# Attention followed by a token and channel mixer on one core: seven block products for the third batch pair's first channel product, thirteen tile pairs, and a new instruction order

## The chip, the cores and the metric

One core of one Trainium2 chip runs the whole program. The time is device microseconds (us) of one execution. The kernel before takes 354.57 us, the median of three runs (353.96 to 354.92). The trace that is read below is one further, profiled execution.

## What is computed

There are 8 batches, 12 heads, 448 rows of the sequence and 64 columns a head. The attention has no softmax: the scores are clipped at zero, squared and multiplied with V. Its output is the input of a mixer: a token product over the sequence with a clip and a second token product, added to the input, then a channel product from 768 to 1536 columns, a clip, and a channel product back to 768, added to its input.

```python
scores = scale * np.matmul(q, k.transpose(0, 1, 3, 2))
attn = np.maximum(scores, 0.0) ** 2 / S
x = attn @ v                                  # heads side by side: (8, 448, 768)
h = np.maximum(x.transpose(0, 2, 1) @ w_tok1, 0.0) @ w_tok2
u = x + h.transpose(0, 2, 1)
out = u + np.maximum(u @ w_ch1, 0.0) @ w_ch2
```

## The kernel before, in words

**Attention** goes over 24 groups of four heads (three groups a batch). A group's K, Q and V come in by six DMAs on the POOL queue (`ldk`, `ldq`, `ldv`, two halves each, line 289), into one of four buffers. K and Q are turned either on TensorE (`T`, groups 0 to 9, with evictions `cp`) or, from group 10 on, by VectorE copies (`ik`, `iq`) and one crossbar transpose on the SP queue (`x`). A score chunk `S{group}.{0..6}` is four 64x64 matmuls (line 431) into two PSUM banks; two evictions `r` clip it (ScalarE at line 267 or VectorE at line 269); one instruction `q` squares it in SBUF (line 441, always VectorE); a value piece `V` is four matmuls (line 458) that accumulate over the seven chunks. Two evictions `xe` close a group.

**Token mixing** of a group turns its rows (on TensorE, `X`, with evictions `xc`, or from group 5 on by a crossbar transpose `xd`, line 481), multiplies twice (`t1`, line 502; `t2`, line 511), with an eviction `rt` between, and adds the group back in (`u`, VectorE, line 515).

**The first channel product** of a batch is twelve products `C1` of six 448-column matmuls (line 565), each evicted and clipped by `c1e` into `r2`, a ring of ten tiles. Two batches make a pair, seven tiles of 128 rows. For the fourth pair (`WIDE = (3,)`) `channel1_wide` computes it in another way: per pair of 128-column blocks seven products `E` of three matmuls (line 645) take the place of the 24 matmuls of two blocks and two batches. It needs four weight sums `sa` (line 609) and four sums of the input `tb` (line 629), both on VectorE. The weight sums are written over the attention's square buffers, `sq_all`, and so wait until the last value piece has read them; the input sums lie over `kqT_all`. Three of the products are saved (`v`, ScalarE or VectorE) and added later (`v` at line 661, with a clip `z`).

**The second channel product** works on tiles of 128 rows. A single tile, `C2`, takes two times twelve matmuls of 384 columns (line 746) and two evictions `c2e` that also add the residual. Two tiles of a pair in `PAIRS` take seven products `D` of six matmuls (line 802) in place of 48, with four sums `ds` (line 788) and seven evictions `de` (lines 773 and 818). The residual, `u` turned back, comes through crossbar transposes `ub` on the SP queue (line 523), but for the batches in `RESPE`, where three 128-column matmuls for each half tile (line 750) add it on TensorE. Stores `st` leave on the SP queue.

**The order** is written out: the string `ORDER` names every step once, and each engine gets its steps in that sequence. `:A` or `:D` puts an eviction on ScalarE or VectorE, digits after a colon are the PSUM banks, `fill:bank*count` is a run of dummy matmuls, and `:g` on a DMA holds a load back until the last crossbar transpose has landed, or a transpose until the last load has. No cost table or due time stands in the kernel.

Of the kernel before, what the change touches and what calls it, by code (L numbers as in the profile page):

```python
# [12 lines left out]
HOLD = 1  # L13
NSIDE = 2
FUSED = set()
# [56 lines left out]
ldk1.1 ldf.1 ldf.0 ldk0.1:g cast1.1:A ldk0.0:g ldq1.1:g cast0.0:A ldk1.0 cast1.0:D ldv0.0 ldq1.0 ident fill:0*21  # L72
T0.1:0 cast0.1:D fill:1*4 T0.0:1 cp0.1:A cp0.0:D ldv0.1 ldk2.1 fill:2*12 S0.0:23 ldq2.0 ldk2.0:g r0.0.0:A S0.2:45
r0.0.1:D r0.2.1:A wt1.0 ldq2.1:g S0.5:67 S0.6:01 r0.5.0:D S0.4:23 q0.0:D S0.1:56 r0.5.1:A r0.2.0:A T1.0:74 r0.1.1:A
r0.6.1:D q0.2:D r0.1.0:A S0.3:16 cp1.1:D r0.4.1:D ldv1.1:g ldv1.0 ldq3.0:g cp1.0:A S1.2:54 r0.6.0:A S1.0:73 q0.1:D
r0.4.0:A r0.3.1:D ldq3.1:g r1.0.1:D r0.3.0:A ldk3.1 fill:0*3 V0.0:02 wt2 V0.1 r1.2.0:A S1.1:16 r1.0.0:A ldk3.0 S1.3:53
q0.5:D r1.1.0:A q0.3:D fill:7*4 S1.4:71 V0.2 r1.3.1:A ldv2.1:g q0.4:D V0.3 wt1.1:g V0.4 q1.0:D r1.2.1:A ldv3.0 S1.6:34
ldv2.0 r1.4.1:A V0.5 r1.1.1:A r1.3.0:A q0.6:D q1.2:D q1.3:D fill:1*5 V0.6 r1.6.1:A r1.6.0:A q1.1:D ldq4.1 r1.4.0:A
T2.0:16 xe0.0:A S1.5:54 cp2.1:A fill:3*5 V1.0:37 xe0.1:A cp2.0:D ldq4.0 V1.1 r1.5.1:A q1.4:D fill:0*8 S2.2:01 r1.5.0:D
V1.2 ldk4.1 r2.2.0:A S2.1:62 r2.2.1:D q1.5:D r2.1.1:A r2.1.0:A q1.6:D V1.3 S2.0:54 r2.0.0:A V1.4 fill:1*6 V1.5 S2.6:10  # L80
r2.0.1:D X0.1:2 X0.0:6 r2.6.1:A V1.6 r2.6.0:A S2.3:54 xc0.1:D S2.4:02 xc0.0:D xe1.1:A T3.0:16 r2.4.1:A ldk4.0 q2.2:D
r2.4.0:D r2.3.1:A wc1.0 q2.0:D X1.1:7 ldv3.1:g xc1.1:A t1.0.1:2 rt0.1:D t1.0.0:0 t1.1.1:4 t2.0.1:7 xe1.0:A cp3.1:D
rt0.0:A t2.0.0:2 q2.1:D u0.1:D r2.3.0:A S2.5:30 q2.4:D cp3.0:A q2.3:D r2.5.0:A ldk5.1 rt1.1:D ldq5.0:g V2.0:65 ldq5.1
V2.1 S3.0:71 r2.5.1:A V2.2 r3.0.0:A r3.0.1:A q2.5:D X1.0:3 q2.6:D V2.3 ldk5.0:g V2.4 xc1.0:A S3.4:07 ldq6.1:g S3.3:41
u0.0:D V2.5 t1.1.0:3 r3.4.0:A V2.6 ldq7.0:g r3.3.1:D T4.0:02 r3.3.0:A rt1.0:A S3.1:43 xe2.1:D xe2.0:A X2.0:1 cp4.0:D
X2.1:6 cp4.1:A t2.1.1:5 xc2.0:D t2.1.0:0 xc2.1:D r3.1.0:A r3.1.1:A u1.1:D t1.2.0:2 t1.2.1:1 wc1.1 ldv4.1:g r3.4.1:A
q3.3:D S4.1:46 rt2.0:A rt2.1:A u1.0:D r4.1.0:A S4.2:35 q3.4:D S3.2:72 r4.2.1:A t2.2.0:1 ldv4.0 u2.0:D t2.2.1:0
r4.2.0:A C1.0.0a:4 u2.1:D S3.5:53 q3.1:D S3.6:10 r3.2.1:A q3.0:D r3.2.0:A r3.5.0:D C1.0.4:2 r3.5.1:A r3.6.1:A C1.0.0
V3.0:73 r4.1.1:A ldq6.0 c1e0.4:A q3.2:D r3.6.0:A S4.3:05 c1e0.0:D V3.1 S4.5:62 r4.3.1:A V3.2 r4.3.0:A T5.0:14 V3.3
q4.1:D S4.4:50 r4.5.0:A cp5.1:A q4.2:D q3.6:D V3.4 q3.5:D C1.0.5:6 V3.5 r4.5.1:D S4.0:42 V3.6 cp5.0:A r4.4.1:D  # L90
ldk7.0:g C1.0.1a:1 C1.0.2a:0 r4.0.1:D ldk6.1:g c1e0.5:D xe3.0:A r4.0.0:D xe3.1:D C1.0.1 r4.4.0:A S4.6:27 S5.2:65
S5.0:43 r4.6.1:A C1.0.2 ldv5.0 q4.0:D r4.6.0:D q4.6:D X3.0:7 r5.0.1:D C1.0.9:2 c1e0.2:A r5.2.1:A C1.0.7:0 V4.0:53
r5.2.0:A c1e0.1:A q4.5:D S5.3:61 r5.0.0:D c1e0.9:D C1.0.11:4 q5.0:D ldk6.0:g V4.1 c1e0.7:A S5.4:20 xc3.0:D r5.3.1:D
# [118 lines left out]
def kernel(ctx: ExitStack, tc: tile.TileContext, q: bass.AP, k: bass.AP, v: bass.AP, moe_w_tok1: bass.AP, moe_w_tok2: bass.AP, moe_w_ch1: bass.AP, moe_w_ch2: bass.AP, out: bass.AP):  # L212
    nc = tc.nc
# [716 lines left out]
```

## Time and profile before

| what | value |
|---|---|
| three runs, median (lowest to highest) | 354.57 us (353.96 to 354.92) |
| the profiled execution's own time | 353.8 us |
| its span | 352.0 us |
| TensorE clock granted | 1.00 throughout |
| TensorE busy | 343.8 us, 98% of the span |
| VectorE busy | 296.0 us, 84% |
| ScalarE busy | 201.0 us, 57% |
| GpSimd busy (it issues the loads) | 91.4 us, 26% |
| DMA moved | 49.85 MB |

The span runs from the first to the last instruction; 1.8 us of the execution lie around it. The profiled execution is 0.8 us below the median of the three runs. PE stands for TensorE's matmuls, PEld for its weight loads, DVE for VectorE, ACT for ScalarE, POOL for GpSimd and SP for the engine that issues most transposes and the stores. A matmul's duration holds its latency, so that what a matmul costs in a stream is read from the start of one to the start of the next, or from a long run of them.

### The profile page before, as it was taken

How to read it: one execution, taken by the hardware profiler on the slowest of the kernel's cores; microseconds unless marked ns; L12 is line 12 of the kernel's file. 1: busy time of each engine (PE TensorE's matmuls, PEld its weight loads, DVE VectorE, ACT ScalarE, POOL GpSimd, SP SyncE). 2: the span in 40 equal slices, each digit the busy share in tenths (PEclk: the TensorE clock that was granted, in tenths of full speed). 3: DMA queues.
4: the chain of work that ended last, by engine and by line, in shares of the span. 5: the costliest groups of instructions: out<-in, count | busy, mean ns of one | idle time of the engine just before them, and what ended most of it. 6: DMA issues, size and time to landing. Idle time of an engine off the chain costs nothing.

```text
span 352.0 us, 8801 instructions
## 1 busy us (share of the span) xinstructions
PE 343.8 (98%) x3547; PEld 190.9 (54%) x3547; DVE 296.0 (84%) x570; ACT 201.0 (57%) x429; POOL 91.4 (26%) x156
## 2 busy tenths in 40 slices
PE   8899999999999999999999999999999999999995
PEld 7475454455565455554555555555545565555563
DVE  2999999889769899897986888879689998968972
ACT  3999879687763586656345237475757621344200
POOL 8883291166046100910244221231000000000000
PEclk9999999999999999999999999999999999999999
DMA  8999999989999998999889997996784540617336
GB/s 150 168 177 188 198 129 196 189 108 150 149 168 168 239 164 112 123 155 174 146 150 203 138 194 108 170 176 91 123 129 40 149 96 4 114 28 165 74 93 167
DMA packets 95626, 49.85 MB, mean 142 GB/s; under 512 B 69536, under 2 KB 92128, under 8 KB 95584
## 3 DMA queue, kind: packets, MB, share of 16 engines
q0 software_dynamic: 24352, 21.47, 43.4%
q1 hardware_dynamic: 70992, 27.60, 43.2%
q8 instruction: 28, 0.46, 0.5%
q10 hardware_dynamic: 240, 0.20, 0.2%
q14 instruction: 14, 0.11, 0.1%
HBM read 43.38 MB, written 11.01 MB: 155 GB/s over the span
## 4 chain that ended last, share of the span: by engine, by line
PE 93%; DVE 2%; DMA 1%; POOL 1%; issue 1%; ACT 0%; POOLq 0%
PE m_ps L565 24%; PE w_ps L802 22%; PE acc_ps L458 10%; PE sc_ps L431 9%; PE w_ps L645 7%; PE t_ps L502 6%; PE m_ps L746 6%; PE h_ps L511 5%; PE kqT_ps L390 1%; DMA x_sb<-xT 1%; POOL raw_all L289 1%; DVE sq_all L441 1%; PE fill_ps L899 1%; PE x_ps L493 1%; DVE sq_all L269 1%
## 5 line engine op out<-in xcount | busy, mean ns | idle before, releaser
L267 ACT ACTIVATE sq_all<-sc_ps 128x448 bf16<-128x448 f32 x243 | 118.3, 566 | 36.2 <-PE sc_ps L431 29.4
L441 DVE TENSOR_TENSOR sq_all<-sq_all 128x896 bf16<-128x896 bf16 x168 | 98.8, 617 | 5.4 <-ACT sq_all L267 5.0
L565 PE MATMUL m_ps<-uT_sb,wc 128*128 128x448 bf16 x432 | 90.3, 353 | 0.0
L269 DVE TENSOR_SCALAR sq_all<-sc_ps 128x448 bf16<-128x448 f32 x93 | 55.8, 618 | 10.0 <-PE sc_ps L431 9.6
L565 PEld LDWEIGHTS <-wc 128*128 128x128 bf16 x432 | 39.9, 98 | 42.3 <-issue 9.1
L458 PE MATMUL acc_ps<-sq_all,raw_all 64*64 64x448 bf16 x672 | 58.3, 357 | 0.2
L431 PE MATMUL sc_ps<-kqT_all 64*64 64x448 bf16 x672 | 53.0, 353 | 1.3 <-ACT kqT_all L273 0.9
L267 ACT ACTIVATE r_sb<-m_ps 128x448 bf16<-128x448 f32 (+3 forms) x78 | 32.8, 451 | 37.3 <-PE m_ps L565 36.9
L289 POOL DMA_DIRECT2D raw_all<-in_v_dram x48 | 29.2, 614 | 69.7 <-DMA u_sb<-uT_sb 22.2
L289 POOL DMA_DIRECT2D raw_all<-in_k_dram x48 | 29.7, 622 | 48.7 <-DMA x_sb<-xT 16.2
L802 PE MATMUL w_ps<-wd,r2d 128*128 128x384 bf16 x198 | 36.8, 326 | 0.0
L289 POOL DMA_DIRECT2D raw_all<-in_q_dram x46 | 28.5, 636 | 31.0 <-DVE side_all L409 19.4
L802 PEld LDWEIGHTS <-r2d 128*128 128x128 bf16 x264 | 25.2, 98 | 19.1 <-issue 2.1
L515 DVE TENSOR_TENSOR uT_sb<-h_ps,xT 128x448 bf16<-128x448 f32 x48 | 29.3, 619 | 6.9 <-PE h_ps L511 6.4
L458 PEld LDWEIGHTS <-raw_all 64*64 64x64 bf16 x672 | 20.0, 105 | 22.0 <-issue 16.1
L431 PEld LDWEIGHTS <-kqT_all 64*64 64x64 bf16 x672 | 23.2, 105 | 15.7 <-issue 6.7
L773 DVE TENSOR_TENSOR out_sb<-w_ps,u_sb 128x384 f32<-128x384 f32 x44 | 23.9, 552 | 7.5 <-PE w_ps L802 7.3
L802 PEld LDWEIGHTS <-r_sb 128*128 128x128 bf16 x198 | 19.0, 98 | 14.4 <-issue 1.8
L746 PE MATMUL m_ps<-wc,r_sb 128*128 128x384 bf16 (+2 forms) x156 | 26.4, 314 | 0.0
L502 PE MATMUL t_ps<-x_sb,wt 128*128 128x256 bf16 (+1 forms) x216 | 24.7, 261 | 0.7 <-DMA x_sb<-xT 0.7
L511 PE MATMUL h_ps<-wt,r_sb 128*128 128x448 bf16 x96 | 24.8, 354 | 0.0
L802 PE MATMUL w_ps<-wc,r_sb 128*128 128x384 bf16 x132 | 24.6, 326 | 0.0
(71 smaller groups left out, 336.6 us busy)
## 6 DMA issues: line engine op xcount, KB each, us to landing
out_dram<-out_sb SPq DMA_DIRECT2D x54, 192.0 KB, 3.2
raw_all<-in_k_dram POOLq DMA_DIRECT2D x48, 112.0 KB, 4.9
raw_all<-in_v_dram POOLq DMA_DIRECT2D x48, 112.0 KB, 4.8
raw_all<-in_q_dram POOLq DMA_DIRECT2D x46, 112.0 KB, 5.2
wc<-in_moe_w_ch_dram POOLq DMA_DIRECT2D x2, 1152.0 KB, 11.2
wc<-in_moe_w_ch_dram POOLq DMA_DIRECT2D x3, 768.0 KB, 12.5
u_sb<-uT_sb SPq DMA_TRANSPOSE x42, 3.2
side_all<-in_q_dram SPq DMA_DIRECT2D x2, 224.0 KB, 3.9
```

What stands on the lines that cost most here:

```text
L267: nc.scalar.activation(out, ps, AF.Relu)
L269: nc.vector.tensor_scalar(out=out, in0=ps, scalar1=0.0, scalar2=None, op0=ALU.max)
L289: return nc.gpsimd.dma_start(out=raws[t][s % NR][64 * half:64 * (half + 1)], in_=src[b, h0:h0 + 2].rearrange('e (p c) d -> p e (c d)', c=KC))
L431: nc.tensor.matmul(o.ps[e][64 * half:64 * (half + 1), :S], lhsT=lhsT, rhs=rhs, start=True, stop=True, skip_group_check=True)
L441: sq_ops[s, c] = [add(Op(f'q{s}.{c}', 'DVE', lambda o: nc.vector.tensor_tensor(out=buf, in0=buf, in1=buf, op=ALU.mult), ev))]
L458: nc.tensor.matmul(o.ps[half][64 * e:64 * (e + 1), :S], lhsT=r[rows, e, c * D:(c + 1) * D], rhs=sq[rows, e, :], start=c == 0, stop=c == KC ...
L502: nc.tensor.matmul(o.ps[:, j, :], lhsT=wt1[:, c, j * 128:(j + 1) * 128], rhs=x_sb[:, p0:p1, c, :], start=c == 0, stop=c == 3)
L511: nc.tensor.matmul(o.ps[:, :S], lhsT=r1[:, j, a * 128:(a + 1) * 128], rhs=wt2[:, j, :], start=j == 0, stop=j == JC - 1)
L515: nc.vector.tensor_tensor(out=uTs[bb % 2][:, 2 * i + a, off:off + S].rearrange('n (c p) -> n c p', c=KC), in0=t2.ps[:, :S].rearrange('n (p ...
L565: nc.tensor.matmul(ps[:, :S], lhsT=wc1[:, g, e * 128:(e + 1) * 128], rhs=uT[:, g, off:off + S], start=g == 0, stop=g == CC - 1)
L746: nc.tensor.matmul(o.ps[:, :size], lhsT=r2[:, e, r2_tile(n)], rhs=wc2[:, e, cols], start=e == 0, stop=e == EC - 1)
L802: nc.tensor.matmul(o.ps[:, :C2], lhsT=lhs[:, e], rhs=rhs[:, e], start=holder is None and e == 0, stop=e == H2 - 1, skip_group_check=True)
```

## The change

Four settings change, and the whole `ORDER` string is new. `WIDE = (2, 3)` gives the third batch pair (batches 4 and 5) the seven block products too: 24 steps `C1` and 24 steps `c1e` go, 42 steps `E2`, four `tb2` and the evictions that belong to them come. Its seven tiles are ready only after all attention. `PAIRS` goes from 11 pairs to 13; the single tiles left are 0 and 27. `RESPE` is empty, so that batch 0's residual comes by six crossbar transposes in place of 18 matmuls on TensorE. `HOLD` and `FUSED` had no effect in the kernel before. A square `q` can now be put on ScalarE; 68 of the 168 are. The dummy matmuls go from 68 to 56.

```diff
-RESPE = {0}
-PAIRS = ((3, 4), (5, 6), (7, 8), (10, 11), (12, 13), (14, 15), (17, 18), (19, 20), (21, 22), (23, 24), (25, 26))
-WIDE = (3,)
+RESPE = set()
+PAIRS = ((1, 2), (3, 4), (5, 6), (7, 8), (9, 10), (11, 12), (13, 14), (15, 16), (17, 18), (19, 20), (21, 22), (23, 24), (25, 26))
+WIDE = (2, 3)
...
-st16.64 sa0:D st13.64 V22.6 V23.6 D17.2:0 rt21.0:A ds17.2:D t2.20.0:7 xe22.1:A sa1:D t2.21.0:1 st15.0 xe22.0:A
+V23.0:14 r23.5.0:A q23.5:D q23.6:A V23.1 V22.6 V23.2 xe22.1:A xe22.0:A V23.3 tb2.0:D V23.4 V23.5 V23.6 st9.64 sa1:D
...
-        sq_ops[s, c] = [add(Op(f'q{s}.{c}', 'DVE', lambda o: nc.vector.tensor_tensor(out=buf, in0=buf, in1=buf, op=ALU.mult), ev))]
+        def square(o):
+            if o.on == 'ACT':
+                nc.scalar.activation(buf, buf, AF.Square)
+            else:
+                nc.vector.tensor_tensor(out=buf, in0=buf, in1=buf, op=ALU.mult)
+        sq_ops[s, c] = [add(Op(f'q{s}.{c}', 'DVE', square, ev))]
...
-        free = [sc[s, c] for s in range(NS - NQ, NS) for c in range(KC)]
+        free = sums_use or [sc[s, c] for s in range(NS - NQ, NS) for c in range(KC)]
...
-            old = hold.get(e - 4, raw_free)
+            old = saved[turn - 4] if turn >= 4 else raw_free
...
-            hold[e] = [ops_of(v2), ops_of(v5), ops_of(v3)]
+            saved.append([ops_of(v2), ops_of(v5), ops_of(v3)])
+            readers += [p4, p5, p6, p7]
+        sums_use[:] = readers
```

The last three pieces let the fourth pair use the input sums' and the saved products' buffers after the third pair.

The order moves at three places that matter below. The first is ScalarE at the start of the program. The names are those of the tiles: `sq_all<-sc_ps` is a clip `r` out of PSUM, `sq_all<-sq_all` a square, `kqT_all<-kqT_ps` an eviction `cp`, `xT<-acc_ps` an eviction `xe`. Before:

```order
L273 ACT_TABLE_LOAD
L273 ACTIVATE raw_all<-side_all 64x448 x2
L273 ACTIVATE kqT_all<-kqT_ps 128x896
L267 ACTIVATE sq_all<-sc_ps 128x448 x6
L273 ACTIVATE kqT_all<-kqT_ps 128x896
L267 ACTIVATE sq_all<-sc_ps 128x448 x14
L468 ACTIVATE xT_64<-acc_ps 128x448
```

And now (the lines of the changed file stand a few further down):

```order
L278 ACT_TABLE_LOAD
L278 ACTIVATE raw_all<-side_all 64x448
L278 ACTIVATE kqT_all<-kqT_ps 128x896
L272 ACTIVATE sq_all<-sc_ps 128x448 x4
L446 ACTIVATE sq_all<-sq_all 128x896
L272 ACTIVATE sq_all<-sc_ps 128x448 x4
L446 ACTIVATE sq_all<-sq_all 128x896
L272 ACTIVATE sq_all<-sc_ps 128x448 x8
L476 ACTIVATE xT_64<-acc_ps 128x448
```

Squares stand between the clips, and one eviction `cp` and one cast have moved to VectorE. One table load stands at the head of either list and there is none further down.

The second place is VectorE around the end of attention, where the weight sums are made (`side_all<-wc` and `sq_all<-wc`, `sa`). `r2d` is the sum buffer of a tile pair, `uT_sb<-h_ps,xT` a step `u`. Before:

```order
L441 TENSOR_TENSOR sq_all<-sq_all 128x896
L609 TENSOR_TENSOR side_all<-wc_69 128x2304
L788 TENSOR_TENSOR r2d_1_92<-r2d_0_91,r_sb 128x768
L609 TENSOR_TENSOR sq_all<-wc_69 128x2304
L788 TENSOR_TENSOR r2d_3_94<-r_sb,r2d_1_92 128x768
L515 TENSOR_TENSOR uT_sb_80<-h_ps,xT_66 128x448
```

And now, with `kqT_all<-uT_sb` the input sums `tb2` and `r_sb<-w_ps,raw_all` the additions to saved products:

```order
L448 TENSOR_TENSOR sq_all<-sq_all 128x896 x6
L637 TENSOR_TENSOR kqT_all<-uT_sb_79 128x1344
L617 TENSOR_TENSOR sq_all<-wc_69 128x2304
L637 TENSOR_TENSOR kqT_all<-uT_sb_79,kqT_all 128x1344
L617 TENSOR_TENSOR sq_all<-sq_all,wc_69 128x2304
L617 TENSOR_TENSOR side_all<-wc_69 128x2304
L670 TENSOR_TENSOR r_sb<-w_ps,raw_all 128x448 x2
```

Before, tile pairs' sums lie between the weight sums, and 60 matmuls of the tile pairs 17 and 19, with the last token products, stand on TensorE between the last value piece and the first `E`. Now the weight sums follow the last squares at once, and TensorE has five products `E` and one `t1` between the last value piece and the first product that needs two weight sums.

The third place is the SP queue at the start. `u_sb<-uT_sb` is a residual transpose `ub`, `x_sb<-xT` a step `xd`, `kqT_all<-side_all` a step `x`. Before:

```order
L343 DMA side_all<-in_q_dram 64x2x448 x2
L481 DMA_TRANSPOSE x_sb_76<-xT_66 128x8x128
L523 DMA_TRANSPOSE u_sb<-uT_sb_79 128x4x128
L481 DMA_TRANSPOSE x_sb_75<-xT_64 128x8x128
L481 DMA_TRANSPOSE x_sb_76<-xT_65 128x8x128
L523 DMA_TRANSPOSE u_sb<-uT_sb_79 128x4x128
L413 DMA_TRANSPOSE kqT_all<-side_all 128x14x128
```

And now:

```order
L348 DMA side_all<-in_q_dram 64x2x448 x2
L489 DMA_TRANSPOSE x_sb_76<-xT_66 128x8x128
L531 DMA_TRANSPOSE u_sb<-uT_sb_79 128x3x128 x4
L489 DMA_TRANSPOSE x_sb_75<-xT_64 128x8x128
L489 DMA_TRANSPOSE x_sb_76<-xT_65 128x8x128
L418 DMA_TRANSPOSE kqT_all<-side_all 128x14x128
L531 DMA_TRANSPOSE u_sb<-uT_sb_79 128x4x128
L531 DMA_TRANSPOSE u_sb<-uT_sb_79 128x3x128 x2
```

Batch 0's residual transposes, of three tiles each, stand ahead of and between the group transposes.

More of the change, by code (lines that the diff above doesn't have):

```diff
@@ L71 @@
 ORDER = """
[L72 to L81, printed above, removed]
@@ L632, in channel1_wide @@
         raw_free = [raw_last[s, t] for s in range(NS - NR, NS) for t in 'kqv']
-        hold = {}
+        readers = []
         for e in range(H2):
-            sv = [raw_all[:, (e % 4 * 3 + i)].rearrange('p e n -> p (e n)').bitcast(FP32) for i in range(3)]
+            turn = len(saved)
+            sv = [raw_all[:, (turn % 4 * 3 + i)].rearrange('p e n -> p (e n)').bitcast(FP32) for i in range(3)]
             ea = slice(e * 128, (e + 1) * 128)
```

274 lines of the change are left out of this document (143 added, 131 removed).

## The prediction

> **What bounds the kernel now.** The page's busy times come first, then who TensorE waited for, then the stretches.
>
> ```profile
> PE 343.8 (98%) x3547; PEld 190.9 (54%) x3547; DVE 296.0 (84%) x570; ACT 201.0 (57%) x429; POOL 91.4 (26%) x156
> ```
>
> ```profile
> PE warm_ps L333 <- DVE warm L330: 1.0, 1, 1.0
> PE sc_ps L431 <- ACT kqT_all L273: 0.9, 1, 0.9
> PE t_ps L502 <- DMA x_sb<-xT: 0.7, 1, 0.7
> PE kqT_ps L390 <- POOL ident masks.py:199: 0.6, 1, 0.6
> PE sc_ps L431 <- ACT sq_all L267: 0.2, 1, 0.2
> PE kqT_ps L390 <- DMA raw_all<-in_k_dram: 0.2, 1, 0.2
> ```
>
> These are all of TensorE's waits for others: 3.6 us of 352. But dummy matmuls and stretched rows hide starvation at the start, so the stretches matter more (columns: length, busy us of PE, PEld, DVE, ACT, POOL, clock, share of the 16 DMA engines, GB/s).
>
> ```profile
> 20.00:40.00 20.00, 19.94 (x417) 12.27 (x414) 19.76 (x40) 19.93 (x46) 10.99 (x18) 1.00 1.14 185
> 40.00:60.00 20.00, 20.00 (x303) 10.02 (x300) 19.67 (x37) 15.87 (x31) 8.81 (x14) 1.00 1.07 166
> 100.00:120.00 20.00, 20.00 (x170) 11.01 (x169) 17.96 (x35) 8.80 (x19) 10.21 (x17) 1.00 1.22 170
> 260.00:280.00 20.00, 20.00 (x188) 10.46 (x187) 18.35 (x35) 14.18 (x35) 0.00 (x0) 1.00 0.53 109
> ...
> 0.00:282.30 282.30, 278.24 (x3152) 152.76 (x3153) 241.16 (x467) 183.80 (x396) 91.39 (x156) 1.00 0.98 154
> 60.00:250.00 190.00, 189.09 (x1772) 101.39 (x1770) 161.09 (x313) 112.34 (x241) 54.75 (x92) 1.00 1.01 155
> ```
>
> So there are two regimes. Up to about 60 us VectorE (19.76 and 19.67 of 20) and, to 40 us, ScalarE (19.93) are full, and TensorE follows them. After that TensorE is the bound, with VectorE at 85% (161.09 of 190) and ScalarE at 59%. The last value pieces are over at 282.3 us.
>
> **Part 1: work that leaves TensorE.** Long runs in the chain of work give the price of a matmul (start, length, line, count).
>
> ```profile
> 235.00 1.95 PE m_ps L746 x12
> 248.59 3.40 PE m_ps L565 x18
> 307.62 3.40 PE w_ps L645 x18
> 326.27 16.58 PE w_ps L802 x102
> ```
>
> A 448-column matmul costs 3.40/18 = 0.189 us, as `C1` or as `E`; a 384-column one 1.95/12 = 16.58/102 = 0.1625 us. The third pair's product goes from 24x6 = 144 to 42x3 = 126 matmuls: 18 x 0.189 = 3.4 us. Two more tile pairs replace four single tiles, 4x24 = 96 matmuls, by 2x42 = 84: 12 x 0.1625 = 1.95 us. The residual matmuls go:
>
> ```profile
> 73.00 0.33 PE L750 MATMUL m_ps<-ident,uT_sb 128*128 128x128 bf16 x3
> 73.17 1.95 PE L746 MATMUL m_ps<-wc,r_sb 128*128 128x384 bf16 x11
> ```
>
> Three of them move the next start by 0.17 us, six such runs by 1.0 us. Sum: 6.4 us less on TensorE, certain as work.
>
> The Trainium skill, TensorE: Matmul & The Clock Gate, section Back-to-back issue gap, speaks against so large a saving: it gives a sustained 131 ns for 512 columns in a stream of weight loads and matmuls. As an estimate from that page the same three terms come to 2.1 + 1.2 + 0.6 = 3.9 us. The trace disagrees, 189 ns for 448 columns over 18 matmuls, so the row stands.
>
> **Part 2: the start.** VectorE and ScalarE set the pace there, so their instructions are counted. Prices, from rows:
>
> ```profile
> L267 ACT ACTIVATE sq_all<-sc_ps 128x448 bf16<-128x448 f32 x243 | 118.3, 566 | 36.2 <-PE sc_ps L431 29.4 <-PE acc_ps L458 5.0 <-ACT sq_all L267 1.2
> L441 DVE TENSOR_TENSOR sq_all<-sq_all 128x896 bf16<-128x896 bf16 x168 | 98.8, 617 | 5.4 <-ACT sq_all L267 5.0
> L273 ACT ACTIVATE kqT_all<-kqT_ps 128x896 bf16<-128x896 bf16 x12 | 11.3, 950 | 0.7 <-PE kqT_ps L390 0.7
> ```
>
> ```profile
> 28.55 1.15 DVE L441 TENSOR_TENSOR sq_all<-sq_all 128x896 bf16<-128x896 bf16 x2
> ...
> 32.06 1.41 ACT L267 ACTIVATE sq_all<-sc_ps 128x448 bf16<-128x448 f32 x3
> ```
>
> In a row, VectorE's squares start 1.15 - 0.62 = 0.53 us apart, ScalarE's clips (1.41 - 0.57)/2 = 0.42 us. No square on ScalarE is in this trace; the nearest row is its copy of the same 896 columns, 0.95 us, less the 0.15 us by which successive ones overlap (0.57 - 0.42): 0.80 us. It could be 0.75 to 0.95.
>
> Up to the first value piece of group 5 the old list puts 90 instructions on VectorE, the new one 98: 6 at 0.53 and 2 short ones at 0.3 more, 3.8 us. ScalarE has 94 and 95; 11 squares come at 0.80, and 7 clips at 0.42, 2 `cp` at 0.80 and a cast at about 0.5 go: 3.7 us more. TensorE has done 2.4 us more by then (the transposition of a group, 8 `X` matmuls, a `t1`, a `t2`, a score chunk). Net 1.4 us later. The same count at the first value piece of group 2 gives 0.9 us, at group 4 3.4 us. I take the mean, **+1.9 us** (0.9 to 3.4).
>
> Ahead of that, `ident` is built after one load in place of seven:
>
> ```profile
> 6.35 0.63 PE L390 MATMUL kqT_ps<-ident,raw_all 64*64 64x64 bf16 x28 [0.56 <-POOL ident masks.py:199]
> ```
>
> That wait of 0.56 us goes; next late is the Q load that the casts wait for, so **-0.4 us** (-0.6 to +0.6, since the loads behind it are reordered too).
>
> **Part 3: attention, groups 15 to 22.** This stretch is squeezed, since the third pair's `C1` no longer pads it. It runs in the trace from
>
> ```profile
> 177.95 0.38 PE L458 MATMUL acc_ps<-sq_all,raw_all 64*64 64x448 bf16 x4
> ```
>
> ```profile
> 277.41 0.38 PE L458 MATMUL acc_ps<-sq_all,raw_all 64*64 64x448 bf16 x4
> ```
>
> 99.5 us. Between the same two value pieces the new list has 132 `C1` matmuls fewer (-24.9), 48 of `C2` and 24 of `D` fewer (-11.7), 9 of `E` more (+1.7), other changes +0.6: 65.2 us for TensorE. VectorE has 126 instructions: 87 at 0.53, 29 of tile pairs at 0.47, 10 side copies at 0.30 (the two rows below, less the same overlap of 0.09) = 62.7 us, 96%. ScalarE has 103 at 0.43 and 19 squares at 0.80 = 59.5 us, 91%. Before they were at 82% and 51%. The nearest row in which TensorE still kept up is 260 to 280 us, 18.35 and 14.18 of 20 (92%, 71%); the one with both full is 20 to 40 us. There TensorE fell behind: from group 2's first value piece to group 5's the list holds 27.0 us of matmuls, and the trace took 28.6, so 1.6 us in 29, or 3.6 in 65. I take **+1.0 us** (0 to 4), nearer to the first row, since VectorE's 96% is nearer to 92%.
>
> ```profile
> L818 DVE TENSOR_TENSOR out_sb<-w_ps,out_sb 128x384 f32<-128x384 f32 x33 | 17.9, 552 | 3.6 <-PE w_ps L802 3.6
> L409 DVE COPY side_all<-raw_all 128x896 bf16<-128x896 bf16 x28 | 10.8, 388 | 2.2 <-DMA raw_all<-in_q_dram 1.9 <-DMA kqT_all<-side_all 0.2
> ```
>
> ```profile
> 26.99 0.55 PE L458 MATMUL acc_ps<-sq_all,raw_all 64*64 64x448 bf16 x8
> ```
>
> ```profile
> 55.58 0.36 PE L458 MATMUL acc_ps<-sq_all,raw_all 64*64 64x448 bf16 x4
> ```
>
> **Part 4: behind attention.** The first product that needs weight sums, `E2.2.6`, waits for `sa1`, `tb2.2` and `sa2`, and these for the last value piece.
>
> ```profile
> L629 DVE TENSOR_TENSOR kqT_all<-uT_sb 128x1344 bf16<-128x1344 bf16 x2 | 1.7, 848 | 0.0
> L609 DVE TENSOR_TENSOR sq_all<-wc 128x2304 bf16<-128x2304 bf16 x1 | 1.4, 1350 | 0.0
> ```
>
> ```profile
> 61.57 0.87 PE t_ps L502 x8
> ```
>
> 1.35 + 0.85 + 1.35, less two overlaps of 0.08, is 3.4 us. TensorE has five products of 3 x 0.189 = 0.57 and a `t1` of 0.87 there, 3.7 us. The cover holds by 0.3 us if VectorE is not late; if it is late by 2 us, 2 us show. **+0.5 us** (0 to 2). The remaining tail, 106 us of TensorE by the same prices, carries 83 us of VectorE; the old tail ran at a like load (56.69 of 68 us from 280 to 348 us) without a wait.
>
> ```profile
> 280.00:348.00 68.00, 67.89 (x430) 39.23 (x428) 56.69 (x106) 17.88 (x35) 0.00 (x0) 1.00 0.42 90
> ```
>
> The 12 dummy matmuls less, `HOLD` and `FUSED` cost nothing: dummies fill waits, the other two had no effect. The six new `ub` join 75 transposes on SP's queue. They stand ahead of `xd6` and behind `xd5`, and wait for batch 0's `u`, which the list has many places earlier, so nothing behind them should be held up; if one were, the `t1` of group 6 would come late by a landing, 3 to 8 us (the row under D), less what it has in hand.
>
> **Sum.** -6.4 + 1.9 - 0.4 + 1.0 + 0.5 = -3.4 us. The profiled execution, 353.8 us, would become 350.4; the median of the runs stands 0.8 above it, so I predict **351.2 us**. All bounds at one end give 348.5 and 358.2; with the terms independent I put this case at 349 to 354.
>
> **Rivals.**
> *B, all of it arrives.* Parts 2 to 4 at their low ends (0.9 - 0.6 + 0 + 0): -6.1 us, 348.5; were the start no later at all, -7.0, 347.6. For it: the table of waits above, 3.6 us in all, at 85% VectorE. Against it: the start is bound by the two engines that get more work.
>
> *C, both eviction engines full.* The two counts of parts 2 and 3 at their high ends: -6.4 + 3.4 - 0.4 + 4.0 + 0.5 = +1.1 us, 355.7. It decides if 96% and 91% behave as the first 60 us did.
> The Trainium skill, ScalarE: Activation LUTs, section Rules for kernel authors, says that relu, max, add and mul belong on VectorE, not ScalarE; its fixed 186 ns and 0.833 ns an element make 0.93 us for a square, an estimate that agrees with the 950 ns row. By that rule each of the 68 moves is a loss; by the rows it is one for ScalarE, 0.80 for 0.53, in a stretch where VectorE would otherwise need 62.7 + 19 x 0.53 = 72.8 us of 65.2.
>
> *D, the DMA engines become the bound: slower.* Up to 282.3 us their share is 0.98, 277 engine-us. Four stores and three `ub` fewer come before the same point, of some 235 transfers, at most 8 us at the mean size; I take 4. But that point moves to 242 us: 27.2 us of `C1` and 16.6 of single tiles no longer come before it, and 3.4 of other steps now do. That asks for 273/242 = 1.13, sustained. The trace has 1.01 over 60 to 250 us and 1.22 in its best 20 us. Shares over 1 are packets that overlap, and whether more would come is not shown. At 1.10 the point comes at 248 us, 6 us late: 357. It decides below 1.13. Against it: transposes still land soon before their readers without a wait, in
>
> ```profile
> DMA to landing us min/median/max: 3.0/4.4/7.7
> ```
>
> for the `x_sb` ones, and TensorE waited once, 0.7 us, for one.
>
> That the change does not do what it says is excluded by the lists: 3487 matmuls for 3547, and one table load.
>
> **Chances.** Forecast 0.52, B 0.20, C 0.12, D 0.16. About 0.3%, 1.06 us, is what a measurement of this kernel can tell from no change. Faster by more: 0.505 + 0.20 + 0.01 + 0.01 = 0.72. Within: 0.015 + 0.055 + 0.03 = 0.10, rounded to 0.11. Slower: C's and D's rest, 0.17. The range leaves out a tenth at each end: 347.6, B's low end, to 356.0, which takes in C and the milder half of D.
>
> **What would show it.** In the changed profile: 18 `E` matmuls still in 3.40 us; the first value piece of group 5 at 57 to 58 us (55.6 before); the last value piece at 242 to 246 us, with VectorE over 92% and ScalarE over 85% from group 15 on, and few us of waits of TensorE for `sq_all`; at most 1 us for the weight sums. Waits of TensorE or VectorE for `raw_all`, `kqT_all` or `x_sb` DMAs of several us would be D. A last value piece at 242 us and no waits would be B.

## The result and the profile after

The changed kernel is slower. It took 369.99 us, the median of four runs, against 354.42 for the kernel before on the same chip; the ratio is 1.033 (95% interval 1.0264 to 1.0396). Its runs differ among themselves by 2% (364.85 to 372.60), where those of the kernel before lie within 0.3%, and the ratio is made from the two faster ones, 364.85 and 367.40. The profiled execution is the one of 364.85 us; its span is 363.1.

The page's busy times and, from the waits, who TensorE waited for:

```profile
PE 345.5 (95%) x3487; PEld 192.0 (53%) x3487; DVE 303.7 (84%) x610; ACT 236.9 (65%) x455; POOL 91.1 (25%) x156
```

```profile
PE sc_ps L436 <- DMA kqT_all<-side_all: 4.0, 2, 3.6
PE h_ps L519 <- DVE sq_all L274: 2.7, 1, 2.7
PE t_ps L510 <- DMA x_sb<-xT: 2.0, 2, 1.7
```

Before, TensorE waited for transfers for 0.9 us. Now it waits 6.0 us for crossbar transposes, and 2.7 for a clip on VectorE that, as the chain below shows, stood behind a load. The stretches show where (length, busy us of PE, PEld, DVE, ACT, POOL, TensorE clock, DMA share, GB/s):

```profile
60.00:160.00 100.00, 98.28 (x1003) 51.83 (x1002) 87.62 (x172) 78.30 (x145) 33.01 (x55) 1.00 1.06 167
0.00:256.00 256.00, 242.68 (x2879) 133.26 (x2880) 218.69 (x429) 207.60 (x391) 91.12 (x156) 0.98 1.01 160
160.00:180.00 20.00, 17.31 (x145) 8.86 (x146) 13.83 (x30) 15.03 (x30) 5.93 (x10) 0.91 1.21 156
180.00:220.00 40.00, 39.96 (x394) 21.82 (x387) 37.13 (x72) 35.14 (x65) 11.25 (x19) 1.00 0.93 153
220.00:240.00 20.00, 14.75 (x137) 7.03 (x135) 12.24 (x26) 12.74 (x26) 1.78 (x3) 0.83 0.87 140
240.00:260.00 20.00, 19.86 (x212) 10.66 (x210) 19.92 (x34) 19.26 (x42) 0.00 (x0) 1.00 0.60 124
260.00:340.00 80.00, 80.00 (x460) 44.67 (x459) 67.30 (x152) 26.01 (x58) 0.00 (x0) 1.00 0.35 71
```

Two holes are seen, 160 to 180 us and 220 to 240 us, in which not only TensorE but VectorE and ScalarE too do less than elsewhere: 13.83 and 12.24 of 20 us on VectorE, against 37.13 of 40 between them. So no engine is the bound there. From 260 us on TensorE is full. The clock that was 1.00 throughout before falls to 0.91 and 0.83.

The chain of work through the two holes (start, length, what):

```profile
145.22 6.58 DMA kqT_all<-side_all
...
153.49 6.54 DMA raw_all<-in_k_dram
...
160.32 7.83 DMA raw_all<-in_k_dram
...
168.25 0.06 DVE side_all L414
...
168.55 0.63 DVE sq_all L274
...
169.22 0.54 PE h_ps L519 x2
...
217.07 6.74 DMA raw_all<-in_v_dram
...
223.83 6.20 DMA kqT_all<-side_all
...
230.07 0.96 PE sc_ps L436 x7
```

In the first, a transpose, two loads one after another and a side copy lead to a clip, and TensorE starts when that has ended: the side copy `ik17` is in VectorE's list ahead of the clip, and it waits for its load.

```profile
DVE side_all L414 <- DMA raw_all<-in_k_dram: 3.7, 1, 3.7
```

In the second, a V load is waited for by a marked transpose (`x21:g`), and that by the scores of group 21. In the whole chain that ended last, transfers now have 18% of the span; the page of before had 1%.

```profile
PE 63%; DMA 18%; ACT 9%; DVE 4%; issue 3%; POOL 2%; SPq 0%; DVEq 0%; POOLq 0%; ACTq 0%
```

Three value pieces mark off the stretches; they are the first ones of groups 5, 15 and 23:

```profile
60.46 0.36 PE L466 MATMUL acc_ps<-sq_all,raw_all 64*64 64x448 bf16 x4
```

```profile
179.41 0.38 PE L466 MATMUL acc_ps<-sq_all,raw_all 64*64 64x448 bf16 x4
```

```profile
254.19 1.14 PE L466 MATMUL acc_ps<-sq_all,raw_all 64*64 64x448 bf16 x20
```

Before they came at 55.58, 177.95 and 277.41 us. From the last of them to the last matmul it takes 104.7 us, as the list gives at the prices used (70.5 us before, with 14 `D` and 39 `E` products more and a few small steps fewer); everything that is lost is lost ahead of it.

### The profile page after: what moved, and what is told of

Its sections match the earlier page's. It is cut to its first block, busy times and chain, and to the rows that moved or that the text cites. A ratio compares the mean times of both kernels' runs of the same rounds, so it can differ in the third digit from the quotient of the medians.

```text
span 363.1 us, 8750 instructions
## 1 busy us (share of the span) xinstructions
PE 345.5 (95%) x3487; PEld 192.0 (53%) x3487; DVE 303.7 (84%) x610; ACT 236.9 (65%) x455; POOL 91.1 (25%) x156
## 4 chain that ended last, share of the span: by engine, by line
PE 63%; DMA 18%; ACT 9%; DVE 4%; issue 3%; POOL 2%; SPq 0%; DVEq 0%; POOLq 0%; ACTq 0%
PE w_ps L813 16%; PE w_ps L654 13%; PE m_ps L573 10%; ACT sq_all L272 6%; PE sc_ps L436 6%; DMA kqT_all<-side_all 5%; PE t_ps L510 4%; DMA raw_all<-in_k_dram 4%; PE acc_ps L466 4%; PE h_ps L519 4%; DMA x_sb<-xT 2%; PE m_ps L757 2%; DMA out_dram<-out_sb 2%; DMA raw_all<-in_v_dram 2%; POOL raw_all L294 2%
## 5 line engine op out<-in xcount | busy, mean ns | idle before, releaser
L272 ACT ACTIVATE sq_all<-sc_ps 128x448 bf16<-128x448 f32 x225 | 110.7, 564 | 23.5 <-PE sc_ps L436 18.3
L274 DVE TENSOR_SCALAR sq_all<-sc_ps 128x448 bf16<-128x448 f32 x111 | 66.2, 618 | 6.0 <-PE sc_ps L436 5.0
L446 ACT ACTIVATE sq_all<-sq_all 128x896 bf16<-128x896 bf16 x68 | 63.6, 958 | 5.6 <-DVE sq_all L274 5.4
L436 PE MATMUL sc_ps<-kqT_all 64*64 64x448 bf16 x672 | 59.7, 363 | 6.6 <-DMA kqT_all<-side_all 4.0
L573 PE MATMUL m_ps<-uT_sb,wc 128*128 128x448 bf16 x288 | 59.9, 353 | 0.0
L448 DVE TENSOR_TENSOR sq_all<-sq_all 128x896 bf16<-128x896 bf16 x100 | 59.3, 618 | 0.7 <-ACT sq_all L272 0.3
L466 PE MATMUL acc_ps<-sq_all,raw_all 64*64 64x448 bf16 x672 | 47.6, 353 | 0.1
L813 PE MATMUL w_ps<-wd,r2d 128*128 128x384 bf16 x234 | 45.1, 332 | 0.0
L573 PEld LDWEIGHTS <-wc 128*128 128x128 bf16 x288 | 26.8, 98 | 26.7 <-issue 3.8
L278 ACT ACTIVATE raw_all<-w_ps 128x448 f32<-128x448 f32 x26 | 13.8, 551 | 33.3 <-PE w_ps L654 30.8
```

The lines of the kernel that those rows point to most:

```text
L272: nc.scalar.activation(out, ps, AF.Relu)
L274: nc.vector.tensor_scalar(out=out, in0=ps, scalar1=0.0, scalar2=None, op0=ALU.max)
L436: nc.tensor.matmul(o.ps[e][64 * half:64 * (half + 1), :S], lhsT=lhsT, rhs=rhs, start=True, stop=True, skip_group_check=True)
L446: nc.scalar.activation(buf, buf, AF.Square)
L448: nc.vector.tensor_tensor(out=buf, in0=buf, in1=buf, op=ALU.mult)
L466: nc.tensor.matmul(o.ps[half][64 * e:64 * (e + 1), :S], lhsT=r[rows, e, c * D:(c + 1) * D], rhs=sq[rows, e, :], start=c == 0, stop=c == KC ...
```

## The experiments

Theory D is the prediction's rival: the DMA engines cannot move what the shorter attention asks of them. Against it stand G (not the engines, but the marks `:g` and the order of the loads hold transfers up), C (VectorE and ScalarE are full) and K (what is lost is the lower clock behind each wait). Intervals are 95%, on the ratio to the kernel before that ran beside it.

**No marks, in either kernel.**

```diff
-ldk5.0:g
+ldk5.0
...
-xd22:g
+xd22
```

> The changed kernel with the mark :g taken off 79 steps, all from the first value piece on, so that no load waits for the last crossbar transpose and no transpose for the last load; the order and the bytes are the same. Theory G (loads and transposes hold each other back: from 60 to 245 us the POOL queue waited 36.0 + 35.1 + 17.9 = 89.0 us for transposes): the stalls of TensorE at 163 to 169 us and 223 to 230 us go, and with them most of the 4.5 and 8 us that it loses around them; 352 to 358 us. Theory D (the DMA engines cannot move the bytes in the time, whatever holds what): 363 us or more, the same stalls a little elsewhere. Theory C (VectorE and ScalarE full): 363 us or more, no change.

> The kernel before with the mark :g taken off the 76 steps from the first value piece on. A control. Theory G: TensorE has 3.6 us of waits there in all, of which 0.9 are for transfers, so that there is next to nothing to win: 353 to 355.5 us. Theory D: the same, or slower by up to 3 us if loads and transposes in flight together cost each other time. A gain of over 2 us would say that the marks cost any order time, and not the changed one alone.

Measured: the changed kernel 1.0714 (1.0632 to 1.0796), some 4% slower than with its marks; the kernel before 1.0316 (1.0239 to 1.0393). G falls in this form. The control missed both of its expectations: 353 to 355.5 us, or up to 3 us more, were expected, and the median was 365.66. The landing times of the transposes `x_sb` say why, first of the changed kernel, then without marks, then of the kernel before without marks (3.0/4.4/7.7 with them):

```profile
DMA to landing us min/median/max: 3.0/3.8/9.0
```

```profile
DMA to landing us min/median/max: 3.0/5.6/11.7
```

```profile
DMA to landing us min/median/max: 3.0/5.6/9.3
```

Transposes and loads that are in flight together slow each other: 1.2 to 1.8 us more for the median one of these transposes. TensorE then waits 15.6 us for transposes in the changed kernel and 10.6 us in the other:

```profile
PE sc_ps L436 <- DMA kqT_all<-side_all: 12.2, 2, 9.5
PE t_ps L510 <- DMA x_sb<-xT: 3.4, 2, 3.1
```

```profile
PE sc_ps L431 <- DMA kqT_all<-side_all: 5.6, 1, 5.6
PE t_ps L502 <- DMA x_sb<-xT: 5.0, 1, 5.0
```

That the kernel before loses 3% when its transfers are merely put beside each other shows that it had little slack in them, although its table of waits looked empty.

**Three marks only**, those at the two holes.

```diff
-ldv16.0:g
+ldv16.0
...
-xd17:g
+xd17
...
-x21:g
+x21
```

> The changed kernel with the mark :g taken off three steps only, those that stood behind its longest stalls: ldv16.0 (held 5 us by group 15's transpose, with the loads of group 17 queued behind it), x21 and xd17 (held by a load that landed at 223.8 us). A narrow form of theory G, since taking off all 79 marks made it slower: the stalls at 169, 225 and 230 us go, 9 us of waits, 355 to 360 us. Theory D: the same transfers then collide or come late elsewhere, 362 to 371 us.

Measured: 1.0353 (1.0290 to 1.0417), unchanged. The chain shows the same transpose of group 21 without its mark:

```profile
221.27 11.09 DMA kqT_all<-side_all
```

It starts 2.6 us sooner than with the mark (223.83) and lands 2.3 us later, after 11.09 us in place of 6.20, among the loads that it no longer waits for. The narrow form of G falls as well. The Trainium skill, DMA: Bandwidth & Descriptors, section Issuing engines are not separate DMA queues, says that transfers issued from SyncE, ScalarE and GpSimd all go over the same 16 engines and interleave there; the two lengths agree with it.

**Six loads moved forward**, with the same bytes.

```diff
-ldk17.0:g V11.4
+ldk17.0:g ldk17.1 V11.4
...
-ldk20.1:g x18:g
+ldk20.1:g ldq21.0 ldq21.1 x18:g
...
-ldq22.0 q18.2:D
+ldq22.0 ldq22.1 ldq23.0 ldk23.1 q18.2:D
```

> The changed kernel with six loads moved forward in the order, to where their buffers have been read already: ldk17.1 behind ldk17.0 (issue at about 135 us in place of 160.3), ldq21.0 and ldq21.1 behind ldk20.1 (178 us for 209.8), ldq22.1, ldq23.0 and ldk23.1 behind ldq22.0 (195 us for 214 to 216); they lose their marks, all else stands. Bytes and their number are the same. If a burst of loads at 155 to 160 and 209 to 218 us, with transposes among them, makes the late transfers: the stalls at 169 and 225 to 230 us shrink by half or more, 354 to 360 us. If the engines cannot move the bytes in the time, whenever they are issued: 362 us or more.

(The places that the loads left are not shown.) Measured: 365.10 us, 1.0322 (1.0276 to 1.0368); the changed kernel's ratio is 1.033. The hole at 169 us is gone, and group 21's scores no longer wait. But TensorE now waits elsewhere, for the transposes of groups 18 and 22 among others:

```profile
PE sc_ps L436 <- DMA kqT_all<-side_all: 9.3, 4, 3.7
```

```profile
186.09 4.34 DMA kqT_all<-side_all
...
226.97 8.82 DMA kqT_all<-side_all
```

The holes move, and the time stays the same. So their place is a matter of the order; mending the order at the holes, here and with the three marks, does not make them smaller.

**Fewer bytes.** The loads were halved in both kernels, the stores cut, and the stores cut with twelve residual transposes.

```diff
-                return nc.gpsimd.dma_start(out=raws[t][s % NR][64 * half:64 * (half + 1)], in_=src[b, h0:h0 + 2].rearrange('e (p c) d -> p e (c d)', c=KC))
+                m = 2 if s < 4 else 1; return nc.gpsimd.dma_start(out=raws[t][s % NR][64 * half:64 * (half + 1), :m], in_=src[b, h0:h0 + m].rearrange('e (p c) d -> p e (c d)', c=KC))
```

> The changed kernel with every load of groups 4 to 23 cut to the first of its two heads (the other head's rows keep what an earlier group left there, so the output is that of other data). 120 loads of 112 KB become 56 KB, 6.7 MB less on the side that is written; the order, the marks and every other instruction stay. Theory D (the DMA engines bind from 60 us on): the stalls of TensorE go, the last value piece comes at 242 to 247 us as forecast, 349 to 353 us. Theory C (VectorE at 96% and ScalarE at 91% hold the stretch whatever the loads do): 360 us or more.

> The kernel before with the same cut of the loads of groups 4 to 23. A control for the run before it: TensorE is busy for 98% there and waits for transfers for 0.9 us. Theory D: 351.5 to 353.5 us, since the padding by C1 of the third pair hides the transfers already. A gain of over 3 us would say that transfers cost the kernel before time as well, and that the forecast read its table of waits wrongly.

Measured: the changed kernel 351.80 us, ratio 0.9932 (0.9902 to 0.9961); the kernel before 352.97 us, 0.9958 (0.9929 to 0.9987). The cut that gives the kernel before 0.4% gives the changed one 4%: with less to move it comes near the 351.2 us that were forecast. Its holes are gone, and the two stretches from 60 us on take about what the sum said:

```profile
61.70 0.36 PE L466 MATMUL acc_ps<-sq_all,raw_all 64*64 64x448 bf16 x4
```

```profile
174.06 0.38 PE L466 MATMUL acc_ps<-sq_all,raw_all 64*64 64x448 bf16 x4
```

```profile
241.49 0.76 PE L466 MATMUL acc_ps<-sq_all,raw_all 64*64 64x448 bf16 x12
```

```profile
0.00:243.00 243.00, 237.84 (x2878) 131.77 (x2878) 218.05 (x428) 206.86 (x391) 82.58 (x156) 0.99 0.87 140
```

```profile
160.00:180.00 20.00, 19.96 (x200) 10.82 (x198) 17.16 (x37) 18.96 (x38) 5.21 (x10) 1.00 0.80 129
220.00:240.00 20.00, 19.86 (x229) 10.65 (x223) 19.95 (x39) 19.97 (x44) 0.77 (x2) 1.00 0.77 137
```

From group 15 to group 23 it is 67.4 us, where 66.2 was forecast and the changed kernel took 74.8. VectorE and ScalarE have exactly the same work in it, and in the last row both are full without TensorE falling behind, so C falls. Like for like the change is now worth 1.2 us (352.97 to 351.80), not the 3.4 forecast. GpSimd, which issues the loads, has less to do in this run too (82.6 us for 91.1); in the next one it has not.

```diff
-                queue.dma_start(out=dst[..., cols], in_=out_sb[p, cols])
+                queue.dma_start(out=dst[..., cols if n > 12 else slice(0, 64)], in_=out_sb[p, cols if n > 12 else slice(0, 64)])
```

> The changed kernel with the stores of tiles 0 to 12 cut to their first 64 of 768 columns (the rest of these rows of the output is not written). 26 stores of 192 KB become 16 KB each: 4.6 of some 38 MB that move up to 245 us are gone, 12%; waits, order and marks are the same. Theory D (demand of 1.13 for a sustained 1.0 to 1.1): the demand falls to 1.0 and the stalls go, 351 to 356 us. Theory G: no store stands between a load and its reader, the same holds remain, 361 to 367 us.

> The changed kernel with the stores of tiles 0 to 12 cut to 64 of 768 columns, and the twelve residual transposes of batches 2 and 3 replaced by transfers of 2 KB, so that these rows of the output are missing or have another residual. No load, side copy or group transpose is touched, nor any mark or the order. Theory D (the DMA engines' load): like the half loads, the stalls behind 160 us go, 350 to 356 us. A rival, that the half loads helped because each load landed 1.2 us sooner (3.5 us for 4.7) on its way to the side copies, the transpose and the scores: as with the small stores alone or worse, 358 to 364 us.

(The diff is that of the stores; the second run has the replaced transposes besides.) Measured: with the small stores 355.84, 360.10, 366.16 and 366.19 us, and the faster two are some 8 us below the changed kernel's faster two; with the residual transposes gone too, 357.95 us, the median of ten, 1.0066 (1.0013 to 1.0118). The DMA share up to 245 us, first of the changed kernel, then with the small stores:

```profile
0.00:245.00 245.00, 231.76 (x2751) 127.69 (x2751) 207.72 (x409) 196.60 (x368) 91.12 (x156) 0.98 1.04 162
```

```profile
0.00:245.00 245.00, 235.60 (x2846) 129.51 (x2846) 216.89 (x426) 205.63 (x388) 91.22 (x156) 1.00 0.98 149
```

No load and no group transpose was touched, GpSimd was as busy as before (91.2 us), and more than half of the loss came back. The kernel before was not run with these cuts; TensorE's waits for transfers there come to 0.9 us. The expectations of 351 to 356 and 350 to 356 us were met by single runs only. The second run gained nothing over the first and lies at the edge of its rival's 358 to 364 us, so a part of what the half loads gave back may come from each load landing sooner. With the residual transposes gone the first hole is still there, 2.2 us of wait behind a K load of 7.46 us, and the clock falls behind it (0.91):

```profile
158.22 7.46 DMA raw_all<-in_k_dram
```

```profile
PE h_ps L519 <- DVE sq_all L274: 2.2, 1, 2.2
```

```profile
160.00:180.00 20.00, 17.76 (x174) 9.71 (x172) 14.33 (x31) 15.73 (x31) 6.14 (x11) 0.91 1.02 148
```

**Dummy matmuls**, first ahead of the waiting steps, then as padding all through the second half of attention.

```diff
+fill:2*30 t2.12.0:2
...
+fill:5*10 t1.13.0:5
...
+fill:1*24 t1.17.0:1
...
+fill:0*40 S21.2:06
```

> The changed kernel with 104 dummy matmuls of 128 columns put ahead of four of the steps at which TensorE waited: 30 ahead of t2.12.0, 10 ahead of t1.13.0, 24 ahead of t1.17.0, 40 ahead of S21.2. They run in the waits (9.9 us in all), and end none of them. Theory K (a part of the loss is TensorE's granted clock, 0.83, 0.90 and 0.75 in the stretches 170 to 180, 220 to 230 and 230 to 240 us): the clock stays at 1.00 to 245 us and 3 to 5 us come back, 360 to 362 us. If the lower clock costs nothing, because TensorE waits for the same transfers anyway: 365 us or a little more.

Measured: 1.0448 (1.0392 to 1.0505), slower by about 1% than the changed kernel, at a mean clock of 0.991 for 0.983. A part of the dummies missed the waits, since the first batch itself waited for its bank behind the side copy:

```profile
PE fill_ps L910 <- DVE sq_all L274: 3.8, 1, 3.8
```

The expectation of K, 360 to 362 us, is missed. So K is not refuted cleanly, but a better clock brought no time.

```diff
-S16.4:43
+fill:4*6 S16.4:43
```

> The changed kernel with 150 dummy matmuls of 128 columns, six at a time ahead of 25 score chunks between the first value pieces of groups 15 and 23, on banks that the chunk takes anyway. At 5.5 us for the 56 dummies of the changed kernel they are 14.7 us of TensorE's time that nothing waits for. Theory D: they stand where it would have waited or run at a lower clock, so that 12 to 15 us of work cost next to nothing, 362 to 371 us. If the transfers are not the limit there: 378 to 382 us.

(The diff shows one of the 25.) Measured: 1.0572 (1.0520 to 1.0625), the median 374.60 us, 8 us over the changed kernel's 364.85 and 367.40, between the two expectations. The first value pieces of groups 15 and 23, with six dummies behind the first:

```profile
180.33 0.38 PE L466 MATMUL acc_ps<-sq_all,raw_all 64*64 64x448 bf16 x4
180.65 0.51 PE L910 MATMUL fill_ps<-warm 128*128 128x128 bf16 x6
```

```profile
264.27 0.95 PE L466 MATMUL acc_ps<-sq_all,raw_all 64*64 64x448 bf16 x16
```

The stretch took 83.9 us. By this row the dummies are 25 x 0.51 = 12.8 us, so that 66.2 + 12.8 = 79.0 us were due without a hole; the excess fell from 8.6 to 4.9 us, and 3.7 of the 12.8 us cost nothing. This is the direction of D, at much less than the size expected. It need not be the transfers alone: the clock stayed at 1.00 from 180 to 260 us, where it had fallen to 0.83, so a part can be the clock's. The hole at 169 us lies ahead of the padding and stayed.

**The start.** 

```diff
-q0.6:A
+q0.6:D
...
-q6.2:A
+q6.2:D
```

> The changed kernel with the eleven squares that ScalarE makes ahead of group 5's first value piece put on VectorE. For the start alone: that value piece came at 60.5 us in the changed kernel, 55.6 before, where +1.9 was counted. If the squares on ScalarE are what makes it late (0.96 us each against 0.53, and two changes of engine): 1 to 3 us earlier there. If both engines are simply full: VectorE has 11 x 0.53 = 5.8 us more, and it comes 2 to 4 us later. The whole time moves by as much or less, 362 to 371 us, since the stalls behind it remain.

(The first and the last of the eleven.) Measured: 1.0503 (1.0415 to 1.0591); the first value piece of group 5 came 4.1 us later, as expected for two full engines, and the median, 373.19 us, lies above the 362 to 371 expected:

```profile
64.55 0.36 PE L466 MATMUL acc_ps<-sq_all,raw_all 64*64 64x448 bf16 x2
```

Both engines are full there, and in this order the moves to ScalarE are a gain.

**Parts alone.** Four runs tried parts of the change, or its main effect, by themselves.

```diff
-for g in gs:
+for g in gs[:1] if b in (4, 5) else gs:
...
```

> The kernel before with each C1 product of the third pair (batches 4 and 5) cut to its first matmul of six, so that those two batches' channel output is wrong. 120 matmuls of 0.189 us, 22.7 us, leave TensorE in the second half of attention; every other instruction, every transfer and the order are those of before. Theory D (this padding gave the transfers their time): not all of it arrives, TensorE waits several us for kqT_all, x_sb or raw_all, the last value piece ends at 264 to 270 us instead of 259.5, and the time is 336 to 345 us. If the new order alone is to blame: 331 to 333 us, without a wait for a transfer of over 1 us.

> The kernel before with C1 of the third pair cut to one matmul of six (as in the run of 346.8 us) and with the half loads of groups 4 to 23; two batches' channel output and the heads left out are wrong. Theory D, that the transfers took what did not arrive of the 22.7 us: 331 to 336 us. A rival, that VectorE did, with 82% of 99.5 us = 82 us of work in a stretch that the cut would make 77 us long: 342 to 347 us, no gain from the transfers.

Measured: 346.83 us, 0.9799 (0.9754 to 0.9843), of 22.7 us 7 arrive; with half loads 346.49 us, 0.9749 (0.9681 to 0.9817), no gain from the transfers. The first seemed to speak for D, and the second takes that back: VectorE is the likelier limit there, as the stretch from 200 to 260 us shows for the two in turn (56.20 and 56.17 of 60 us on VectorE):

```profile
200.00:260.00 60.00, 53.65 (x492) 26.72 (x491) 56.20 (x113) 35.08 (x81) 11.23 (x19) 1.00 0.94 154
```

```profile
200.00:260.00 60.00, 54.90 (x508) 26.65 (x507) 56.17 (x111) 38.41 (x89) 8.61 (x17) 0.97 0.75 131
```

All squares are VectorE's in that kernel. This pair says nothing on D; it suggests that the 68 squares on ScalarE had to come with the shorter attention.

```diff
-WIDE = (2, 3)
+WIDE = (3,)
```

> The changed kernel with one part undone: the third pair's first channel product in its old form. The 42 E2 steps, four tb2 and their evictions go; 24 C1 and 24 c1e come back, spread from group 16 to the end of attention, and PSUM banks are chosen anew from there to the first products of the fourth pair. The 13 tile pairs, the crossbar residual and the rest of the new order stay. TensorE's list is 3.4 us longer. Theory D (only the squeeze of the second half of attention makes the transfers late): no stall of over 1 us after 180 us, 351 to 356 us. A rival, that the new order is at fault wherever it stands (the stalls at 169 us come ahead of the padding): 360 us or more.

Measured: 387.01 us, 1.0911 (1.0839 to 1.0983). That is in the rival's range, and D's sign was missed too: TensorE waits once for 2.6 us for an `x_sb` transpose behind 180 us. But TensorE loses time behind attention as well, where no load is left (17.32 and 17.65 us busy of 20 from 320 to 360 us). The banks chosen anew are the likely cause, which is not shown, and the time says nothing on the theories.

```diff
-RESPE = {0}
+RESPE = set()
...
+PAIRS = ((1, 2), (3, 4), (5, 6), (7, 8), (9, 10), (11, 12), (13, 14), (15, 16), (17, 18), (19, 20), (21, 22), (23, 24), (25, 26))
```

> The kernel before with two parts of the change alone: the pairs (1, 2), (9, 10), (11, 12), (13, 14) and (15, 16) in place of (10, 11), (12, 13), (14, 15) and the single tiles 1, 2, 9 and 16, and batch 0's residual by six crossbar transposes. The third pair keeps its 24 C1; PSUM banks are chosen anew from the first new pair on. By the sum's terms TensorE's list is 1.95 + 1.0 = 3.0 us shorter. Theory D: with the padding kept the saving arrives, 350.5 to 352.5 us. A rival, that six more transposes and seven more VectorE steps a pair early in attention cost as much: 353 us or more.

> Once more the kernel before with the pairs (1, 2), (9, 10), (11, 12), (13, 14), (15, 16) in place of (10, 11), (12, 13), (14, 15) and four single tiles, and with batch 0's residual by crossbar; the third pair keeps its 24 C1. The order behind the first 450 steps was put together anew, with some clips moved between ScalarE and VectorE. TensorE's list is 3.0 us shorter. If the padding is what matters: 350.5 to 353 us. If the new order of the transfers costs by itself, as in the first attempt: 358 us or more.

Measured: 1.0784 (1.0667 to 1.0902) and 1.0539 (1.0430 to 1.0648). Both orders lose 19 us and more where 3.0 should be won. Both fall to their rival, but these orders are not that of the changed kernel, so what the tile pairs and the crossbar residual are worth by themselves, or cost, stays open. No version beat the kernel before with the whole computation in it.

## Why the prediction was wrong, point by point

The forecast for the profiled execution was 350.4 us, and it took 364.85: 14.5 us more, and slower where faster was forecast.

**Part 1, the work that leaves TensorE, was right.** The changed kernel runs `E` at the price used, and so does TensorE in the tail:

```profile
258.01 3.40 PE w_ps L654 x18
```

The rule of the Trainium skill with its 131 ns (TensorE: Matmul & The Clock Gate, section Back-to-back issue gap) did not hold here either; 189 ns for 448 columns did. The prediction's estimate from it scales the 131 ns down to 128 columns for its third term, 0.6 us, which goes beyond the figure it rests on; the row used in the sum, 1.0 us, is the measured one.

**Part 2, the start, was right in its prices and 1 us short.** The square costs what its nearest row said, 0.96 us with its latency:

```profile
L446 ACT ACTIVATE sq_all<-sq_all 128x896 bf16<-128x896 bf16 x68 | 63.6, 958 | 5.6 <-DVE sq_all L274 5.4
```

Group 5's first value piece came 4.9 us later, of which 2.4 are the work that the new list has done by then: 2.5 net, for 1.9 - 0.4 = 1.5 forecast. (The 57 to 58 us given as a sign left those 2.4 out; by its own terms it should have read 59.5, and 60.46 was measured.) The squares moved to ScalarE are worth 4.1 us there, against the rule of the Trainium skill quoted under C.

**Part 3 is the step that failed.** It costed the squeezed attention by VectorE and ScalarE alone and gave +1.0 us; transfers had no term in the sum, and the ten groups ahead of it (5 to 14) none at all. Measured: between the first value pieces of groups 5 and 15 the new list has about 10 us less than the old one (two single-tile steps in place of six, 24 matmuls of tile pairs more, 12 of `C1`, 16 of `t1`, the 18 of the residual and one group's transposition fewer), so that 122.4 - 10 = 112.4 us were due, and 118.9 passed: 6.5 lost. From group 15 to 23 it was 74.8 for 66.2: 8.6 lost. With the loads halved the same two stretches took 112.4 and 67.4 us. That shows the terms for the engines to have been right to some 2 us (like for like the change was worth 1.2 us there and not 3.4), and the missing one to be the transfers.

**Part 4 was right.** The weight sums cost nothing that shows: from group 23's first value piece on it took 104.7 us, and TensorE was full from 260 to 340 us.

**Rival D, with a chance of 0.16, was the case that came**, in that transfers became the limit, though neither its demand nor its price was right. It asked 273 engine-us by the last value piece, at 242 us. That value piece came at 256 us, and by then the engines had given 256 x 1.01 = 259 us in the changed kernel, and 256 x 1.02 = 261 in the kernel before:

```profile
0.00:256.00 256.00, 251.94 (x2894) 139.37 (x2895) 216.61 (x423) 166.16 (x353) 91.39 (x156) 1.00 1.02 158
```

The two shares are nearly equal, with the whole of TensorE's padding in the one and none in the other: the changed kernel asked for 259/242 = 1.07 and got what the old one had, not the 1.10 with which D was priced, nor the 1.22 of the best 20 us. That 1.02 is a fixed limit is not shown. In the first hole the share was 1.21, and without the marks it was 1.06 over the same 256 us, with fewer bytes moved (155 GB/s for 160) and a longer time:

```profile
0.00:256.00 256.00, 231.90 (x2751) 126.43 (x2751) 207.48 (x409) 196.11 (x369) 91.17 (x156) 0.97 1.06 155
```

So the share also rises where transfers slow each other, and both demand and limit are softer than D's working has them. What spoke against D in the prediction, transposes that land before their readers without a wait, is no sign of slack: while TensorE is 98% busy, a transfer that is just in time and one with time in hand look the same.

**What was not counted: the clock.** Behind the waits the rows show TensorE at half speed for a while. The same 8 matmuls of `t1` behind the first hole and in the tail:

```profile
170.81 1.82 PE t_ps L510 x8
```

```profile
257.14 0.87 PE t_ps L510 x8
```

0.91 over 20 us is 3.6 us at half clock, 0.83 is 6.8. In the second hole the clock fell at about 228.5 us, while TensorE still waited until 230.07, so that 1.6 of the 6.8 us cost nothing. That leaves about 1.8 and 2.6 us of matmul time, an estimate from these rows. The Trainium skill, TensorE: Matmul & The Clock Gate, section What's actually happening, has the clock at half behind an idle window of about 3.4 us until an equally long busy one; the 3.6 and 6.8 us, one and two such windows, agree with it. The section HAM oscillation of the same page of the Trainium skill speaks of idle gaps of over 3.4 us. Here a wait of 2.7 us was enough, and in the run with relieved engines one of 2.2; another of 2.7 us in that run, ahead of 230.5 us, left the clock at 1.00. How much of the 14.5 us the clock makes by itself was not separated: the dummies raised it and brought no time.

What stays open is the split: stores and residual transposes gone gave back 8 to 9 us, half loads all but some 2 us of it (like for like), and half loads both relieve the engines (a share of 0.87 for 1.04) and land sooner (a median of 3.5 us for 4.7). The runs above show that the loss shrinks with what has to be moved, and that mending the order at the holes does not shrink it (taking off all marks made it larger). That the engines' load alone, without the shorter landing, would bring back all is not shown.

## What to carry to other kernels

When work that pads a stretch is taken out, every resource that it hid gets less time, and the transfers belong in the sum beside the engines: take the bytes or engine-us that must have moved by the end of the stretch, and divide by the share that the old kernel sustained over all of it, not by its best slices. This warns and does not price: with D's 273 and 1.02 it gives 268 us, where 256 were measured. A table of waits that is empty under a full engine says nothing about how near the next bound is; a run that makes its transfers slower does (3.2% lost without the marks), while halving the loads, which showed it at once in the changed kernel, gained only 0.4% in the old one. And if a hole moves when the order is mended, and does not shrink, look for what sets the sum.

## What the runs showed of the hardware that was not expected

Loads and crossbar transposes in flight together cost each other more than the holding back costs: 3.2% of the kernel before and some 4% of the changed one. One transpose took 11.09 us among loads and 6.20 behind them.

TensorE's clock fell to half behind single waits of 2.2 and 2.7 us, for about 3.6 us; behind another wait of 2.7 us it did not.
